# Block-sparse attention and an MLP in one kernel: the first loads, the sparse mask and the register load are given to other engines

## The chip, the cores and the metric

The kernel runs on one core of a Trainium2 chip. The metric is the time of one execution on the device, in microseconds (us); smaller is better. The core has TensorE (PE in the profile), VectorE (DVE), ScalarE (ACT), GpSimd (POOL) and SyncE (SP), which here does nothing but issue transfers (DMAs). Each engine runs its own instructions in the order of its program and waits on semaphores for the others. DMAs are issued by SyncE, GpSimd and, in the changed kernel, ScalarE.

## The reference

Four batches with eight heads each, 768 positions, 64 numbers per head. The positions are cut into 24 blocks of 32. A block of queries sees its own block and its two neighbours, the first and the last block, and three blocks drawn at random (`sampled_blocks`, 24 x 3). The first and the last block of queries see everything. The attention's output, 3072 tokens of 512 numbers, goes through an MLP.

```
scores = scale * q @ k.T                       # per batch and head, 768 x 768
mask   = window of 1 block | first, last block (rows and columns) | sampled blocks
attn   = softmax(where(mask, scores, -1e9))
x      = attn @ v                              # 3072 tokens x 512
r      = maximum(x @ w_in, 0)                  # 2048 wide
out    = (s * r * r + b) @ w_out               # 3072 x 512, f32
```

The inputs are in double precision; the kernel reads their words and, for the MLP's weights, takes the numbers apart on the chip (`decode_f64`).

## The kernel before, in words

**Order of the work.** The kernel first lists its steps as operations, `op(engine, cost, priority, function, ...)`, with what each needs, and a class `Plan` (line 109) then plays through them with a planned cost for each and writes every engine's program in the order in which the operations would start. The table `START` holds when an engine is assumed to begin, the table `T` due times. So a changed cost, priority or engine moves instructions far from the edit, while the work done stays the same.

**Two halves.** Index `e` is 0 or 1: each half takes two batches (a = 0, 1), with a key tile `kt0` or `kt1`. In each half the rows of queries are handled in slots: a dense slot (first and last block of queries, against all keys) and sparse sets 4s, 0s, 3s, 5s, 1s, 2s (the tile names `qr_4s` and so on; `qr_0d` holds the dense queries of a half). A query tile is loaded by four DMAs of 128 KB (`load_q`, line 711): two batches a by two halves par of the partitions. There are four buffers for query tiles. Sparse scores don't multiply with `kt` but with `kk`, a small tile of gathered key blocks, which GpSimd copies from `kt` (lines 894, 896, 905: window and global blocks; line 907: sampled blocks, at an address in a register).

**A slot.** TensorE multiplies queries and keys into a bank of scores (s, line 941 dense, line 962 sparse). VectorE takes scores, mask and the row's maximum (line 980, result nm). ScalarE takes the exponential (line 993). TensorE transposes the result (t, lines 1021 and 1023), VectorE or ScalarE copy it out (lines 1031, 1033, 1039, 1041), and TensorE multiplies with the values (xs, line 1089; od, line 1079) from tiles `vA` and `vB`, which SyncE and GpSimd load block by block (lines 769, 782 window blocks; 875, 879 sampled blocks).

**First loads.** SyncE loads the sampled numbers (`sbi`, line 808), four pieces of the keys (`kt`, line 703, 384 KB each), two of the four dense query loads (line 717), the other four pieces, the other two dense queries, and then values. GpSimd loads sparse queries: all four loads of a set before the key copies of its slot.

**Sampled numbers.** VectorE turns them into f32 (`sbf`, line 814) and packs the three of a query block into one word (`sparse_indices`, `packed`). GpSimd makes the mask of sampled blocks that the window or another sampled block already covers (`sparse_sampled`, 17 operations, shown as line 106, into `iv` and `mt`). SyncE and GpSimd then load the 22 words into registers (`load_registers`, line 850, one TENSOR_LOAD), and `block_register` shifts and masks one block number out of a word.

**In the middle.** While the attention runs, the MLP's weights `w_in` and `w_out` come in as `raw_i` and `raw_o` and are decoded in steps (lines 85 to 95: `wkhp`, `wklp`, `win`) that the plan puts between the others.

Of the kernel before, what the change touches and what calls it, by code (L numbers as in the profile page):

```python
# [19 lines left out]
P = 128  # L20
NEG = -float(2.0 ** 33)
# [87 lines left out]
class Plan:  # L109
# [7 lines left out]
    START = {"p": 1390.0, "a": 4000.0, "v": 2800.0, "g": 2130.0, "s": 600.0}  # L117
# [95 lines left out]
def kernel(  # L213
# [21 lines left out]
    NB = 24  # L235
# [430 lines left out]
    with ExitStack() as es:  # L666
# [44 lines left out]
        def load_q(key, a, par):  # L711
            kind, e, t = key
            if key not in qts:
                qts[key] = qp.tile([P, 2, NPAIR, P], F32, tag="qr", name=f"qr{e}_{t}{kind}")
            rows, b = slice(par * D, (par + 1) * D), 2 * e + a
            src = q_dup[b, t, rows, par::2, :] if kind == "s" and t < NSP else q_edge[b, int(kind == "d"), rows, par::2, :]
            (nc.gpsimd if kind == "s" else nc.sync).dma_start(out=qts[key][rows, a], in_=src)
# [86 lines left out]
        box = {}  # L804

        def load_sampled():
            box["sbi"] = ptp.tile([P, 4 * P], I32, tag="pt", name="sbi")[:, :2 * NB * NSL]
# [8 lines left out]
        packed = pers.tile([P, NB], I32, name="packed")  # L816

        def sparse_indices(V):

            cl = pers.tile([P, NB * NSL], F32, name="cl")  # L820
            V.tensor_scalar(out=cl, in0=sbf.rearrange("p a b -> p (a b)"), scalar1=0.0, scalar2=float(NB - 1), op0=ALU.max, op1=ALU.min)
            cv = cl.rearrange("p (n a) -> p n a", a=NSL)
            for a in range(1, NSL):
                V.scalar_tensor_tensor(out=cv[:, :, 0], in0=cv[:, :, a], scalar=float(NB32 ** a), in1=cv[:, :, 0], op0=ALU.mult, op1=ALU.add)
            V.tensor_copy(packed, cv[:, :, 0])

        iv = pers.tile([P, NB - 2, NSL], F32, name="iv")

        def sparse_sampled(G):

            t2 = pers.tile([P, NB - 2, NSL], F32, name="t2")
# [8 lines left out]
            for a in range(NSL):  # L840
                for c in range(a):
                    G.tensor_tensor(out=t2[:, :, 0], in0=sp[:, :, a], in1=sp[:, :, c], op=ALU.subtract)
                    G.tensor_scalar(out=t2[:, :, 0], in0=t2[:, :, 0], scalar1=0.0, scalar2=None, op0=ALU.is_equal)
                    G.tensor_tensor(out=iv[:, :, a], in0=iv[:, :, a], in1=t2[:, :, 0], op=ALU.add)
            G.tensor_scalar(out=mt[:, 1:NB - 1, 1:2 * NSL:2], in0=iv, scalar1=1.0, scalar2=NEG, op0=ALU.min, op1=ALU.mult)
# [3 lines left out]
        def load_registers(eng):  # L849
            _, regs[eng] = nc.values_load_multi_w_load_instructions(  # L850
                packed[0:1, 1:NB - 1], engines=[eng], min_val=0, max_val=NB32 ** NSL - 1, bass_reorder=False,
                skip_runtime_bounds_check_because="three numbers of 0..NB-1, clamped on the chip")

        def block_register(eng, k, a):

            n = regs[eng][k - 1] >> (5 * a) if a else regs[eng][k - 1]
            return (n & (NB32 - 1) if a < NSL - 1 else n).with_bounds(min_val=0, max_val=NB - 1)
# [298 lines left out]
        o_rg = op("g", 4800, T["RS"] - 2.0, lambda: load_registers(mybir.EngineType.Pool), [o_si])
# [23 lines left out]
        first_pk = first_q = pq = pvl = pvs = pk = o_m = o_e = o_rc = o_ev = None  # L1180
# [5 lines left out]
        for i, (kind, e, k, r) in enumerate(slots):  # L1186
# [4 lines left out]
            def queries(which=(0, 1), after=None):  # L1191
                nonlocal pq, first_q
                if which[0] in lqs.setdefault(qk, {}):
                    return
                if not dense:
                    first_q = first_q or qk
                for a in which:
                    for par in range(2):
                        fresh = not (a or par)
                        pq = op("s" if dense else "g", 450 if dense else 700, max(u - T["QL"], -18.0 if dense else -4.5) + 0.01 * par + (9.5 * (u == 0) if dense else 0.02) * a,  # L1200
                                lambda qk=qk, a=a, par=par: load_q(qk, a, par), alloc=[("qr", qk)] if fresh else [], use=[] if fresh else [("qr", qk)],
                                order=[pq] if dense else [pq, after, o_rg if first_q in (None, qk) else first_pk], nbytes=131e3)
                        lqs[qk].setdefault(a, []).append(pq)
# [412 lines left out]
```

## Time and profile before

| what | us |
|---|---|
| median of three runs | 764.71 |
| lowest and highest run | 760.99, 767.12 |
| span of the profiled execution, first to last instruction | 766.4 |
| TensorE busy in it | 739.7 |
| VectorE, ScalarE, GpSimd busy | 566.4, 475.0, 284.8 |

The profiled execution's own time is its span; the page gives nothing around it. Attention fills roughly the first 240 us, the MLP the rest. In the profile a group of equal instructions is one row: start, length, engine and line, operation, output and inputs, count; in square brackets stands the idle time of the engine just ahead of it and what ended it. "SPq" and "POOLq" are the engines' instruction queues, where the issue of a DMA shows.

### The profile page before, as it was taken

Reading aid. Unit: us, or ns where it says so; the run is one execution under the profiler, and the core shown is the slowest. Engines: PE = TensorE matmul, PEld = TensorE weight load, DVE = VectorE, ACT = ScalarE, POOL = GpSimd, SP = SyncE. Lnnn points to the kernel's source line nnn. Section 1 sums busy time; section 2 is a strip of 40 time slices with the busy share of each in tenths; the row PEclk is TensorE's granted clock in tenths of the full one; section 3 lists DMA queues with packets and bytes.
Section 4 is the critical chain, followed back from the end, with each engine's and each line's share of the span. In section 5 each row is a group of like instructions: output and inputs, shape, how many; then the busy total and the mean of one; then the engine's idle time right before and its main releaser. Section 6 shows DMA issues by size and latency. Waiting matters only on the chain.

```text
span 766.4 us, 21414 instructions
## 1 busy us (share of the span) xinstructions
PE 739.7 (97%) x8032; PEld 627.8 (82%) x8032; DVE 566.4 (74%) x1436; ACT 475.0 (62%) x1141; POOL 284.8 (37%) x477
## 2 busy tenths in 40 slices
PE   8899998999898999999999999999999999999997
PEld 6576676677677999998878899888888998888896
DVE  4766676988686898887896788796778678666652
ACT  3766677888686887879654444575444467345443
POOL 4866677566751221121032232233222232222221
PEclk9899999999999999999999999999999999999999
DMA  8787877756675335535532221224000022000002
GB/s 263 215 234 251 248 209 223 205 181 204 205 207 143 110 128 175 165 112 145 137 103 77 83 90 62 63 69 124 1 1 1 1 62 83 1 1 0 1 1 82
DMA packets 98743, 89.41 MB, mean 117 GB/s; under 512 B 50352, under 2 KB 79664, under 8 KB 98640
## 3 DMA queue, kind: packets, MB, share of 16 engines
q1 hardware_dynamic: 92544, 71.40, 31.1%
q0 software_dynamic: 6096, 16.65, 7.7%
q8 instruction: 63, 1.03, 0.6%
q14 instruction: 40, 0.33, 0.1%
HBM read 69.15 MB, written 14.68 MB: 109 GB/s over the span
## 4 chain that ended last, share of the span: by engine, by line
PE 80%; DVE 6%; ACT 5%; DMA 4%; issue 3%; SPq 1%; POOL 1%; POOLq 0%; ACTq 0%; DVEq 0%
PE m L622 20%; PE o L486 10%; PE o L487 10%; PE o L485 10%; PE xs L1089 5%; PE t L1023 5%; PE s L962 5%; PE h L443 3%; PE h L445 3%; PE h L444 3%; PE od L1079 2%; PE t L1104 2%; ACT ptile L993 1%; PE t L1021 1%; DVE ptile L980 1%
## 5 line engine op out<-in xcount | busy, mean ns | idle before, releaser
L464 POOL TENSOR_TENSOR hid<-hid,hid 128x384 fp32r<-128x384 f32 x96 | 105.6, 1101 | 292.6 <-ACT hid L640 248.9
L639 ACT ACTIVATE hid<-hid,sb_b,sb_s 128x384 f32<-128x384 f32 x96 | 68.0, 709 | 151.5 <-DVE hid L633 151.4
L993 ACT ACTIVATE ptile<-ptile,nm 128x256 f32<-128x256 f32 (+1 forms) x208 | 107.3, 520 | 35.3 <-DVE nm L980 35.2
L980 DVE CUSTOM_DVE_ANT_1 ptile<-s,mt 128x256 f32<-128x256 f32 x176 | 64.7, 420 | 28.0 <-PE s L962 27.8
L487 PE MATMUL o<-woutr,hid 128*128 128x512 f32 x168 | 66.5, 396 | 0.0
L486 PE MATMUL o<-woutr,hid 128*128 128x512 f32 x168 | 66.3, 395 | 0.0
L485 PE MATMUL o<-woutr,hid 128*128 128x512 f32 x168 | 65.3, 389 | 0.0
L622 PE MATMUL m<-wout,win 128*128 128x384 f32 x264 | 62.2, 339 | 1.1 <-ACT xrest L1509 0.6
L622 PE MATMUL m<-xp,wop 128*128 128x384 f32 x288 | 58.3, 337 | 0.0
L1023 PE MATMUL t<-ident,ptile 128*128 128x128 f32 x352 | 56.4, 301 | 1.6 <-issue 1.5
L486 PE MATMUL o<-win,hid 128*128 128x512 f32 x144 | 57.3, 398 | 0.0
L622 PE MATMUL m<-xp,win 128*128 128x384 f32 x288 | 55.7, 340 | 1.4 <-DVE xp L606 0.7
L633 DVE SCALAR_TENSOR_TENSOR hid<-hid 128x384 f32<-128x384 f32 x96 | 54.3, 566 | 3.3
L622 PEld LDWEIGHTS m<-xp,win 128*128 128x128 f32 x288 | 51.3, 189 | 4.6 <-DVE xp L606 1.2
L640 ACT CAST hid<-hid 128x384 fp32r<-128x384 f32 x96 | 49.3, 514 | 7.8 <-PE o L487 0.4
L1023 PEld LDWEIGHTS t<-ident,ptile 128*128 128x128 f32 x352 | 46.6, 209 | 8.8 <-issue 3.3
L622 PEld LDWEIGHTS m<-xp,wop 128*128 128x128 f32 x288 | 51.5, 188 | 2.1
L622 PEld LDWEIGHTS m<-wout,win 128*128 128x128 f32 x264 | 47.5, 188 | 3.5 <-ACT xrest L1509 1.0
L487 PE MATMUL o<-win,hid 128*128 128x512 f32 x126 | 50.1, 397 | 0.0
L485 PE MATMUL o<-win,hid 128*128 128x512 f32 x126 | 49.7, 394 | 0.2
L907 POOL COPY kk<-kt 128x256 f32 x132 | 49.8, 406 | 0.0
L1089 PE MATMUL xs<-vA,pt 128*32 128x64 f32 x1696 | 47.0, 227 | 2.1 <-DVE pt L1039 1.4
(195 smaller groups left out, 1868.1 us busy)
## 6 DMA issues: line engine op xcount, KB each, us to landing
vB<-in_v_dram SPq DMA_DIRECT2D x76, 128.0 KB, 3.7
raw_o<-in_w_out_dram SPq DMA_DIRECT2D x14, 512.0 KB, 3.3
raw_i<-in_w_in_dram SPq DMA_DIRECT2D x12, 512.0 KB, 3.8
vA<-in_v_dram POOLq DMA_DIRECT2D x46, 128.0 KB, 3.6
xd<-xst SPq DMA_DIRECT2D x44, 128.0 KB, 4.1
vA<-in_v_dram SPq DMA_DIRECT2D x42, 128.0 KB, 3.9
out_dram<-ob SPq DMA_DIRECT2D x20, 256.0 KB, 2.0
sum<-xd SPq DMA_DIRECT2D x12, 384.0 KB, 4.6
```

The lines of the kernel that those rows point to most:

```text
L464: (eng or nc.vector).tensor_tensor(out=htile(5 + i % 3), in0=t, in1=gh.bitcast(F32), op=ALU.subtract)
L485: nc.tensor.matmul(acc, gh[:, tsl], wout(f, 0), start=first, stop=False)
L486: nc.tensor.matmul(acc, gh[:, tsl], wout(f, 1), start=False, stop=False)
L487: nc.tensor.matmul(acc, gl[:, tsl], wout(f, 0), start=False, stop=last)
L622: nc.tensor.matmul(to, w_, x_, start=(c == 0 and k == 0), stop=(c == 1 and k == 2))
L633: vec.scalar_tensor_tensor(out=t, in0=t, scalar=0.0, in1=t, op0=ALU.max, op1=ALU.mult)
L639: nc.scalar.activation(t, t, AF.Identity, bias=sb_b, scale=sb_s)
L907: nc.gpsimd.tensor_copy(flat(kg[:, a:a + 1]), flat(kts[e][:, bass.ds(j, 1)]))
L980: nc.vector.tensor_tensor_reduce(out=pt, in0=sp, in1=msk, scale=-scale, scalar=FMAX if g == 0 else nm[:, 0:1], op0=ALU.add, op1=ALU.min, a ...
L993: nc.scalar.activation(pt, pt, AF.Exp, bias=nms[n][:, last:last + 1], scale=-1.0, accum_out=dns[i][:, g, j:j + 1])
L1023: nc.tensor.transpose(tp[:, (2 * j + c) * P:(2 * j + c + 1) * P], src[:, c:SW:2], ident)
L1089: nc.tensor.matmul(xs[quads[pair]], pt[:, c, quads[pair]], vt[:, a, col:col + D], start=(j == 0 and c == 0), stop=(c == 1), tile_position= ...
```

## The change

Five edits. `load_q` is told which engine issues: ScalarE the dense queries of the first half and the first sparse set, SyncE the dense queries of the second half, GpSimd the rest. Six block numbers instead of three stand in one word (`packs`), so that the register load reads 11 words. The mask is split: `sparse_near` (7 operations) stays on GpSimd, `sparse_same` (4) and `sparse_mask` (2) go to VectorE. GpSimd's queries of the next two sets get a priority and an order ahead of the key copies. `START["a"]`, the time from which the plan counts ScalarE as free, and planned costs are changed.

```
-    START = {"p": 1390.0, "a": 4000.0, "v": 2800.0, "g": 2130.0, "s": 600.0}
+    START = {"p": 1390.0, "a": 2400.0, "v": 2800.0, "g": 2130.0, "s": 600.0}
...
-        def load_q(key, a, par):
+        def load_q(key, a, par, on):
...
-            (nc.gpsimd if kind == "s" else nc.sync).dma_start(out=qts[key][rows, a], in_=src)
+            {"a": nc.scalar, "g": nc.gpsimd, "s": nc.sync}[on].dma_start(out=qts[key][rows, a], in_=src)
...
+        first = ptp.tile([P, 4 * P], I32, tag="pt", name="sbi")
+        box["sbi"], at_ = first[:, :2 * NB * NSL], [2 * NB * NSL]
...
-        packed = pers.tile([P, NB], I32, name="packed")
+        packed = room(NB)
+        packs = pers.tile([P, NB // 2 - 1], I32, name="packs")
...
+            V.scalar_tensor_tensor(out=packs, in0=packed[:, 2:NB - 1:2], scalar=5 * NSL, in1=packed[:, 1:NB - 2:2], op0=ALU.logical_shift_left, op1=ALU.bitwise_or)
...
-        def sparse_sampled(G):
+        def sparse_near(G):
...
-            for a in range(NSL):
-                for c in range(a):
-                    G.tensor_tensor(out=t2[:, :, 0], in0=sp[:, :, a], in1=sp[:, :, c], op=ALU.subtract)
-                    G.tensor_scalar(out=t2[:, :, 0], in0=t2[:, :, 0], scalar1=0.0, scalar2=None, op0=ALU.is_equal)
-                    G.tensor_tensor(out=iv[:, :, a], in0=iv[:, :, a], in1=t2[:, :, 0], op=ALU.add)
-            G.tensor_scalar(out=mt[:, 1:NB - 1, 1:2 * NSL:2], in0=iv, scalar1=1.0, scalar2=NEG, op0=ALU.min, op1=ALU.mult)
+        def sparse_same(V):
+            sp = sbf[:, 1:NB - 1]
+            V.tensor_tensor(out=same[:, :, 1:], in0=sp[:, :, 1:], in1=sp[:, :, :1].broadcast_to([P, NB - 2, 2]), op=ALU.subtract)
+            V.tensor_tensor(out=same[:, :, 0], in0=sp[:, :, 2], in1=sp[:, :, 1], op=ALU.subtract)
+            V.tensor_scalar(out=same, in0=same, scalar1=0.0, scalar2=None, op0=ALU.is_equal)
+            V.tensor_tensor(out=same[:, :, 2], in0=same[:, :, 2], in1=same[:, :, 0], op=ALU.add)
+        def sparse_mask(V):
+            V.tensor_tensor(out=iv[:, :, 1:], in0=iv[:, :, 1:], in1=same[:, :, 1:], op=ALU.add)
+            V.tensor_scalar(out=mt[:, 1:NB - 1, 1:2 * NSL:2], in0=iv, scalar1=1.0, scalar2=NEG, op0=ALU.min, op1=ALU.mult)
...
-                packed[0:1, 1:NB - 1], engines=[eng], min_val=0, max_val=NB32 ** NSL - 1, bass_reorder=False,
+                packs[0:1], engines=[eng], min_val=0, max_val=NB32 ** (2 * NSL) - 1, bass_reorder=False,
...
-            n = regs[eng][k - 1] >> (5 * a) if a else regs[eng][k - 1]
-            return (n & (NB32 - 1) if a < NSL - 1 else n).with_bounds(min_val=0, max_val=NB - 1)
+            n, at = regs[eng][(k - 1) // 2], a + (k - 1) % 2 * NSL
+            n = n >> (5 * at) if at else n
+            return (n & (NB32 - 1) if at < 2 * NSL - 1 else n).with_bounds(min_val=0, max_val=NB - 1)
...
-        o_rs = op("s", 4400, T["RS"], lambda: load_registers(mybir.EngineType.SP), [o_si])
-        o_rg = op("g", 4800, T["RS"] - 2.0, lambda: load_registers(mybir.EngineType.Pool), [o_si])
+        o_rs = op("s", 2400, T["RS"], lambda: load_registers(mybir.EngineType.SP), [o_si])
+        o_rg = op("g", 2600, T["RS"] - 2.0, lambda: load_registers(mybir.EngineType.Pool), [o_si])
...
+                on = "a" if qk in (("d", 0, 0), first_q) else "s" if dense else "g"
+                soon = sum(x[0] == "s" for x in lqs) <= 3
...
-                        pq = op("s" if dense else "g", 450 if dense else 700, max(u - T["QL"], -18.0 if dense else -4.5) + 0.01 * par + (9.5 * (u == 0) if dense else 0.02) * a,
-                                lambda qk=qk, a=a, par=par: load_q(qk, a, par), alloc=[("qr", qk)] if fresh else [], use=[] if fresh else [("qr", qk)],
-                                order=[pq] if dense else [pq, after, o_rg if first_q in (None, qk) else first_pk], nbytes=131e3)
+                        pq = pqs[on] = op(on, {"s": 450, "a": 620, "g": 650}[on], max(u - T["QL"], -18.0 if dense else -9.0 if soon else -4.5) + 0.01 * par + 0.02 * a,
+                                lambda qk=qk, a=a, par=par, on=on: load_q(qk, a, par, on), alloc=[("qr", qk)] if fresh else [], use=[] if fresh else [("qr", qk)],
+                                order=[pqs.get(on)] if on != "g" else [pqs.get(on), after, o_rg if soon else first_pk], nbytes=131e3)
```

TensorE's program is the same before and after, row by row. The other engines' programs change at these places.

ScalarE at its start, before. `ptile` is the tile of exponentials, `nm` the negated maximum, and L993 the exponential:

```order
L790 ACT_TABLE_LOAD
L790 ACTIVATE warm_108<-ident_101 128x1 [waits Pool_49]
L993 ACTIVATE ptile2_79,dn0_262<-ptile2_79,nm0_249 128x128x3 [waits DVE_49]
L993 ACTIVATE ptile6_80,dn0_262<-ptile6_80,nm0_249 128x128x3
L993 ACTIVATE ptile6_80,dn0_262<-ptile6_80,nm1_259 128x128x3 [waits DVE_49]
```

And after, where L1010 is the exponential; DMAHW0 to DMAHW7 are the eight semaphores that the DMAs of SyncE and ScalarE use in turn (`sbi` has 0, the key pieces have 1 to 7 and then 0):

```order
L790 ACT_TABLE_LOAD
L790 ACTIVATE warm_108<-ident_101 128x1 [waits Pool_49]
L717 DMA qr0_0d_134<-in_q_edge_dram 64x4x128 [waits DMAHW1_49]
L717 DMA qr0_0d_134<-in_q_edge_dram 64x4x128 [waits DMAHW2_49]
L717 DMA qr0_0d_134<-in_q_edge_dram 64x4x128 [waits DMAHW4_49]
L717 DMA qr0_0d_134<-in_q_edge_dram 64x4x128 [waits DMAHW5_49]
L717 DMA qr0_4s_170<-in_q_dup_dram 64x4x128 [waits DMAHW6_49]
L717 DMA qr0_4s_170<-in_q_dup_dram 64x4x128 [waits DMAHW0_49]
L717 DMA qr0_4s_170<-in_q_dup_dram 64x4x128 [waits DMAHW1_49]
L717 DMA qr0_4s_170<-in_q_dup_dram 64x4x128 [waits DMAHW2_49]
L1010 ACTIVATE ptile2_79,dn0_252<-ptile2_79,nm0_238 128x128x3 [waits DVE_49]
```

Eight DMA instructions, each with a wait, stand ahead of ScalarE's first exponential.

GpSimd in the middle, before, around the load of `qr1_0s` (the second half's 0s queries) and the weight copies `wklp`:

```order
L879 DMA vB_232<-in_v_dram 32x2x512
L717 DMA qr1_0s_2607<-in_q_dup_dram 64x4x128 x4
L782 DMA vA_231<-in_v_dram 32x2x512
L894 COPY kk_301<-kt1_590 128x256
L896 COPY kk_301<-kt1_590 128x768
```

And after, from the window copy that follows the three slots' first copies:

```order
L896 DMA vA_161<-in_v_dram 32x2x512
L913 COPY kk_278<-kt1_522 128x256
L922 COPY kk_278<-kt1_522 128x256
...
L924 COPY kk_278<-kt1_522 128x256
L88 COPY wklp0_524<-raw_o0_2450 128x512
L717 DMA qr1_0s_3036<-in_q_dup_dram 64x4x128 x4
L717 DMA qr1_3s_3059<-in_q_dup_dram 64x4x128 x4
```

The second half's 0s and 3s queries have moved behind the first slots' key copies and behind the copy `wklp<-raw_o`.

VectorE in the middle, before, where `xss` closes a slot and L980 is the maximum of the next dense slot:

```order
L1031 TENSOR_SCALAR dp_2715<-t_0_2699,kept 128x4x128
L1095 TENSOR_TENSOR xss_2732<-od_796,rc_452 128x128
L85 TENSOR_SCALAR wkhp_431<-raw_o_2496 128x512
L980 ISA ptile_80,nm_2748<-s_0_2723,mz 128x128x3
L980 ISA nm_2748 128x1
```

And after, at the same place (L997 is the maximum):

```order
L1048 TENSOR_SCALAR dp_2669<-t_0_2654,kept 128x4x128
L1112 TENSOR_TENSOR xss_2686<-od_756,rc_418 128x128
L93 TENSOR_TENSOR win_2690<-wkhp_396,raw_i_2248 128x512
L997 ISA ptile_80,nm_2700<-s_0_2677,mz 128x128x3
L997 ISA nm_2700 128x1
```

The step on `raw_o` no longer stands there; it comes 44 rows later.

## Rows read from the trace of the kernel before

**Rows 1.** The page's first part: busy time, share of the span and instructions of each engine.

```profile
PE 739.7 (97%) x8032; PEld 627.8 (82%) x8032; DVE 566.4 (74%) x1436; ACT 475.0 (62%) x1141; POOL 284.8 (37%) x477
```

**Rows 2.** Windows of 40 us: the window and its length, busy time of PE, PEld, DVE, ACT and POOL with the number of instructions, the granted TensorE clock, the DMA share and GB/s.

```profile
0.00:40.00 40.00, 33.72 (x360) 24.58 (x368) 24.29 (x88) 21.75 (x64) 27.49 (x77) 0.92 0.81 236
...
120.00:160.00 40.00, 36.26 (x735) 25.94 (x723) 33.55 (x120) 33.05 (x102) 26.09 (x53) 0.96 0.71 203
```

**Rows 3.** Timeline of SyncE's queue: its first load of sampled values.

```profile
23.62 0.64 SPq L879 DMA_DIRECT2D vA<-in_v_dram  x1
```

**Rows 4.** Timeline of VectorE and ScalarE at the start of the dense stage: the first maximum and two exponentials.

```profile
11.86 0.56 DVE L980 CUSTOM_DVE_ANT_1 ptile<-s,mz 128x384 f32<-128x384 f32 x1 [5.77 <-PE s L941]
...
13.23 0.61 ACT L993 ACTIVATE ptile<-ptile,nm 128x384 f32<-128x384 f32 x1 [10.87 <-DVE nm L980]
...
16.07 0.62 ACT L993 ACTIVATE ptile<-ptile,nm 128x384 f32<-128x384 f32 x1 [0.28 <-DVE nm L980]
```

**Rows 5.** Timeline of TensorE in the dense stage and around 34 us.

```profile
10.84 2.80 PE L941 MATMUL s<-kt,qr_0d 64*64 64x384 f32 x28 [1.24 <-DMA qr_0d<-in_q_edge_dram]
...
17.22 1.74 PE L941 MATMUL s<-kt,qr_0d 64*64 64x384 f32 x16
...
21.61 1.78 PE L941 MATMUL s<-kt,qr_0d 64*64 64x384 f32 x16
...
32.21 0.76 PE L962 MATMUL s<-kk,qr_3s 64*32 64x256 f32 x16
34.54 1.56 PE L962 MATMUL s<-kk,qr_3s 64*32 64x256 f32 x16 [1.57 <-DMA qr_3s<-in_q_dup_dram]
36.03 1.93 PE L1089 MATMUL xs<-vA,pt 128*32 128x64 f32 x64
37.89 1.98 PE L1023 MATMUL t<-ident,ptile 128*128 128x128 f32 x8
```

**Rows 6.** The chain that ended last, in order of time, from 26 to 48 us: start, length, what.

```profile
28.41 6.09 DMA qr_3s<-in_q_dup_dram
...
41.72 1.03 PE xs L1089 x64
...
43.83 1.15 PE t L1023 x8
```

**Rows 7.** Windows, columns as in rows 2.

```profile
4.00:18.00 14.00, 12.06 (x95) 9.60 (x93) 6.22 (x23) 4.49 (x14) 6.19 (x19) 1.00 1.10 323
34.00:40.00 6.00, 5.46 (x96) 3.87 (x104) 2.89 (x12) 1.20 (x6) 4.07 (x11) 0.50 0.74 215
130.00:132.00 2.00, 2.00 (x33) 0.76 (x21) 1.60 (x6) 0.82 (x4) 0.15 (x1) 0.50 0.39 93
```

**Rows 8.** Timeline of VectorE, GpSimd and TensorE around 128 us.

```profile
127.29 0.43 DVE L85 TENSOR_SCALAR wkhp<-raw_o 128x512 int32<-128x512 int32 x1 [2.71 <-DMA raw_o<-in_w_out_dram]
127.64 0.55 DVE L980 CUSTOM_DVE_ANT_1 ptile<-s,mz 128x384 f32<-128x384 f32 x1
...
127.32 1.01 POOL L88 COPY wklp<-raw_o 128x512 uint16<-128x512 uint16 x1 [0.20 <-DMA raw_o<-in_w_out_dram]
...
128.34 0.64 PE L962 MATMUL s<-kk,qr_2s 64*32 64x256 f32 x8 [1.64 <-POOL wklp L88]
129.59 1.93 PE L962 MATMUL s<-kk,qr_2s 64*32 64x256 f32 x24 [0.62 <-DVE nm L980]
...
131.86 1.60 PE L1089 MATMUL xs<-vA,pt 128*32 128x64 f32 x64
```

**Rows 9.** Timeline of GpSimd: four query loads of the front, a value load, and the loads of the second half's 0s queries.

```profile
22.29 2.44 POOL L717 DMA_DIRECT2D qr_0s<-in_q_dup_dram  x4
...
38.08 0.55 POOL L782 DMA_DIRECT2D vA<-in_v_dram  x1 [1.40 <-PE xs L1089]
...
119.79 2.47 POOL L717 DMA_DIRECT2D qr_0s<-in_q_dup_dram  x4 [0.83 <-PE t L1104]
```

**Rows 10.** The tiles kt and qr_0d in the first 20 and 30 us, and line 850, the register load: instructions with their least, median and greatest duration in ns and first and last start; and the time from a DMA's issue to its landing (the first such row is that of kt, the second that of qr_0d).

```profile
L703 SPq DMA_DIRECT2D kt<-in_k_blk_dram x8: 422/578/2332, 1.3 to 9.9; - x8
...
DMA to landing us min/median/max: 4.7/5.7/6.9
...
L717 SPq DMA_DIRECT2D qr_0d<-in_q_edge_dram x4: 603/846/1092, 5.3 to 12.5; - x4
...
DMA to landing us min/median/max: 4.6/5.4/5.4
...
L850 POOLq TENSOR_LOAD <-packed x1: 5151/5151/5151, 11.2 to 11.2; - x1
```

**Rows 11.** Timeline of GpSimd and TensorE from 139 to 153 us.

```profile
139.69 0.39 POOL L896 COPY kk<-kt 128x256 f32<-128x256 f32 x1 [2.33 <-PE s L962]
...
140.37 1.09 POOL L907 COPY kk<-kt 128x256 f32 x3
...
146.66 1.46 PE L962 MATMUL s<-kk,qr_0s 64*32 64x256 f32 x32
...
151.68 1.09 PE L962 MATMUL s<-kk,qr_3s 64*32 64x256 f32 x32
```

**Rows 12.** The tiles qr_0s and qr_3s from 110 to 140 us: the time from issue to landing of the second half's loads (the first row is that of qr_0s).

```profile
DMA to landing us min/median/max: 5.1/5.2/5.3
...
DMA to landing us min/median/max: 3.8/3.8/3.8
```

More of the change, by code (lines that the diff above doesn't have):

```diff
@@ L804, with room @@
         box = {}
+        first = ptp.tile([P, 4 * P], I32, tag="pt", name="sbi")
+        box["sbi"], at_ = first[:, :2 * NB * NSL], [2 * NB * NSL]
+        def room(n):
+            at_[0] += n
+            return first[:, at_[0] - n:at_[0]]
         def load_sampled():
-            box["sbi"] = ptp.tile([P, 4 * P], I32, tag="pt", name="sbi")[:, :2 * NB * NSL]
             nc.sync.dma_start(
@@ L814, in sampled_blocks @@
             V.tensor_copy(sbf.rearrange("p a b -> p (a b)"), box["sbi"].rearrange("p (n two) -> p n two", two=2)[:, :, 0])
-        packed = pers.tile([P, NB], I32, name="packed")
+        packed = room(NB)
+        packs = pers.tile([P, NB // 2 - 1], I32, name="packs")
         def sparse_indices(V):
-            cl = pers.tile([P, NB * NSL], F32, name="cl")
+            cl = room(NB * NSL).bitcast(F32)
             V.tensor_scalar(out=cl, in0=sbf.rearrange("p a b -> p (a b)"), scalar1=0.0, scalar2=float(NB - 1), op0=ALU.max, op1=ALU.min)
@@ L825, in sparse_indices @@
             V.tensor_copy(packed, cv[:, :, 0])
+            V.scalar_tensor_tensor(out=packs, in0=packed[:, 2:NB - 1:2], scalar=5 * NSL, in1=packed[:, 1:NB - 2:2], op0=ALU.logical_shift_left, op1=ALU.bitwise_or)
         iv = pers.tile([P, NB - 2, NSL], F32, name="iv")
-        def sparse_sampled(G):
-            t2 = pers.tile([P, NB - 2, NSL], F32, name="t2")
+        same = room((NB - 2) * NSL).bitcast(F32).rearrange("p (n a) -> p n a", a=NSL)
+        def sparse_near(G):
+            t2 = room((NB - 2) * NSL).bitcast(F32).rearrange("p (n a) -> p n a", a=NSL)
             sp, own = sbf[:, 1:NB - 1], jf[:, 1:NB - 1].unsqueeze(2).broadcast_to([P, NB - 2, NSL])
@@ L850, in load_registers @@
             _, regs[eng] = nc.values_load_multi_w_load_instructions(
-                packed[0:1, 1:NB - 1], engines=[eng], min_val=0, max_val=NB32 ** NSL - 1, bass_reorder=False,
-                skip_runtime_bounds_check_because="three numbers of 0..NB-1, clamped on the chip")
+                packs[0:1], engines=[eng], min_val=0, max_val=NB32 ** (2 * NSL) - 1, bass_reorder=False,
+                skip_runtime_bounds_check_because="six numbers of 0..NB-1, clamped on the chip")
         def block_register(eng, k, a):
-            n = regs[eng][k - 1] >> (5 * a) if a else regs[eng][k - 1]
-            return (n & (NB32 - 1) if a < NSL - 1 else n).with_bounds(min_val=0, max_val=NB - 1)
+            n, at = regs[eng][(k - 1) // 2], a + (k - 1) % 2 * NSL
+            n = n >> (5 * at) if at else n
+            return (n & (NB32 - 1) if at < 2 * NSL - 1 else n).with_bounds(min_val=0, max_val=NB - 1)
         ring = {"k": {}, "v": {}}
@@ L1147, in chain @@
             for step in later.steps:
-                dep = op(eng, cost, prio, step, [dep])
+                dep = op(eng, cost, prio, step, [dep], use=[("pt", "sbi")])
             return dep
         o_si = chain("v", nc.vector, 250, T["SI"], sparse_indices, o_sb)
-        o_ss = chain("g", nc.gpsimd, 270, T["MS2"], sparse_sampled, o_sb)
-        o_rs = op("s", 4400, T["RS"], lambda: load_registers(mybir.EngineType.SP), [o_si])
-        o_rg = op("g", 4800, T["RS"] - 2.0, lambda: load_registers(mybir.EngineType.Pool), [o_si])
+        o_sn = chain("g", nc.gpsimd, 330, T["MS2"], sparse_near, o_sb)
+        o_sd = chain("v", nc.vector, 200, T["SI"] + 0.1, sparse_same, o_sb)
+        o_ss = op("v", 450, T["SI"] + 0.2, lambda: sparse_mask(nc.vector), [o_sn, o_sd], use=[("pt", "sbi")])
+        o_rs = op("s", 2400, T["RS"], lambda: load_registers(mybir.EngineType.SP), [o_si])
+        o_rg = op("g", 2600, T["RS"] - 2.0, lambda: load_registers(mybir.EngineType.Pool), [o_si])
         kld = {}
@@ L1179 @@
         devs, drc, done, late, held, pav = {}, {}, {}, {}, set(), None
-        first_pk = first_q = pq = pvl = pvs = pk = o_m = o_e = o_rc = o_ev = None
+        pqs = {}
+        first_pk = first_q = pvl = pvs = pk = o_m = o_e = o_rc = o_ev = None
         lastk = {}
@@ L1191, in queries @@
             def queries(which=(0, 1), after=None):
-                nonlocal pq, first_q
+                nonlocal first_q
                 if which[0] in lqs.setdefault(qk, {}):
```

## The prediction, made before the changed kernel was run

> **What bounds the kernel now.** I read the page's busy times first: TensorE works 739.7 us of a span of 766.4 us [rows 1]. In stretches of 40 us it works 33.72 us of the first and 36.26 of the fourth [rows 2]. So a microsecond that TensorE loses anywhere is a microsecond of the end, and a faster loading front counts only as far as it takes idle time or the lower clock away from TensorE. The timelines of those two stretches then show three losses.
>
> First, the start. The first dense scores run at 10.84, 1.24 us after the warm-up ended [rows 5], and ScalarE, idle for 10.87 us, begins its first exponential at 13.23 [rows 4]. From there the dense stage goes at the pace of ScalarE and VectorE.
>
> Second, the stop at 33 us. The second half of the first qr_3s scores waits 1.57 us for its query load, issued by GpSimd as late as 28.41 behind the key copies [rows 5, 6]. The granted clock is then 0.50 from 34 to 40 us, the 1.2 GHz level [rows 7]. That costs more than the wait: 1.56 us for 16 scores that take 0.76 before it, 1.93 for 64 xs and 1.98 for 8 t that take 1.03 and 1.15 a few us later [rows 5, 6], together 0.80 + 0.90 + 0.83 = 2.5. The place loses 1.6 + 2.5 = 4.1 us.
>
> Third, 127 us. VectorE stands 2.71 us at wkhp<-raw_o, a step of the MLP weight decoding, until a load lands; the maxima of the next dense slot are queued behind it. TensorE waits 1.64 and 0.62 us [rows 8] and runs at a clock of 0.50 again [rows 7].
>
> **The change, part by part.**
>
> *ScalarE issues eight query loads.* All stand in its in-order program ahead of the first exponential. The order printed for the changed program says what each waits for: eight DMA semaphores are used in turn by the loads of SyncE and ScalarE, and a load takes its semaphore only when the load before it on that one has landed. Counted off, sbi has 0, key pieces 1 to 7 have 1 to 7, and key piece 8, which itself waits for sbi, has 0 again. ScalarE's fourth dense load therefore waits for the fifth key piece, the first qr_4s load for the sixth, and the second qr_4s load, on semaphore 0, for the eighth and last. That a DMA instruction holds its engine while it waits is seen on GpSimd: a vA load at 38.08 has 1.40 us of idle time ahead of it, put down to TensorE's xs [rows 9]. So the first exponential starts after the last key piece has landed, plus three issues.
>
> The Trainium skill says the same: by "DMA: Bandwidth & Descriptors", section "Anatomy of one DMA — SWDGE (gpsimd) path", DMA engines do not wait on semaphores; the issuing sequencer waits before it dispatches. The trace agrees, by the 1.40 us of GpSimd just named.
>
> When does that piece land? From 4 to 18 us the engines moved 323 GB/s at a DMA share of 1.10 [rows 7]: issuing earlier finds no free transfer time. Before, the last key issue starts at 9.9 and a piece lands after 4.7 to 6.9 us [rows 10], so at 14.6 to 16.8. After, ahead of its landing go 8 keys of 0.393 MB, sbi 0.074, four dense queries of 0.131, one qr_4s of 0.131, one vA of 0.131: 4.0 MB, and of GpSimd's eight early loads 0 to 0.7 MB. At 0.323 MB/us from 4 us on, 4.0 to 4.7 MB end at 16.4 to 18.6. I take 17, and as the early end 15.6, with keys, sbi and dense queries alone. ScalarE has issued no DMA in the trace; GpSimd's issues take 0.61 each (2.44 for four) [rows 9], SyncE's dense queries up to 1.09 [rows 10]. I take GpSimd's, since by then no key is left to issue: 17 + 0.1 + 3 x 0.62 = 19.0, against 13.23. That is +5.8 us (+4.3 from 15.6 and 0.61, +8.7 from 18.6 and 1.09). Whether the first scores come a little earlier is then worth nothing: what follows them waits for the exponentials.
>
> The rule against this part stands in the Trainium skill, page "DMA: Bandwidth & Descriptors", section "Issuing engines are not separate DMA queues": several issuing engines save only the sequencer's issue time. The DMA share of 1.10 agrees. By it alone the sum of this part would be about 0, not +5.8; the waits make the difference.
>
> Two small terms follow. VectorE is by then ahead, so the 0.28 us that ScalarE waited at 16.07 [rows 4] goes: -0.3. And TensorE, its score banks full after some 3 us, stands still for about 6; no row shows so long a stop, and after the 1.57 us at 34 the clock fell. From one dense slot's 16 scores to the next are 4.4 us (17.22 to 21.61 [rows 5]), in which TensorE has little idle time; at half clock a slot is up to 4 us longer. The half clock at 34 held for some 6 us: I take half a slot's price, +2 (0 if the clock doesn't fall, +4 for a whole slot).
>
> *GpSimd loads qr_0s and qr_3s ahead of the copies; mask on two engines; short register load.* Before, GpSimd's load of 22 words begins at 11.2, behind 17 mask operations, and takes 5.15 us [rows 10]. With ten operations fewer it begins no later; 11 words take an estimated 2.6, eight issues 4.9, so the last is out by 18.7 and, with the 6.1 us of [rows 6], landed by 24.8, long before the qr_3s scores, which stood at 32 and come some 8 us later. The wait and its clock go: -4.1 (0 if another wait takes the place). The key copies begin with the last key piece at 17 or behind these issues; one slot's copies fit between the end of its four issues (22.29 + 2.44 [rows 9]) and 28.41, where the next set is already being issued [rows 6], so three take under 11 us and end by 30, wanted one slot after the other from about 33 on: hidden. VectorE's six mask operations lie in its 5.77 us before the first maximum [rows 4]: hidden. SyncE's vA and sampled loads now wait for qr_4s to land, near 22; its first sampled load went out at 23.62 [rows 3], so little is late.
>
> Front: +5.8 - 0.3 + 2 - 4.1 = +3.4.
>
> *The middle, moved by the plan.* The other engines' programs are reordered, TensorE's is the same row by row. At VectorE's place of wkhp<-raw_o stands win<-wkhp,raw_i, which waits for no load but those of the first keys; the raw_o step comes 44 rows later. VectorE was free at 124.58 (127.29 less 2.71), so with one step ahead the dense maxima start at about 125.6 instead of 127.64, the x24 scores near 127.4 instead of 129.59 (-2.2), and without half clock they take 0.8 (24 of the 32 in 1.09 us of [rows 11]) instead of 1.93 and the next 64 xs 1.03 instead of 1.60 [rows 6, 8]: -1.1 - 0.6. Sum -3.9 (0 if win waits as long; -4.4 if no idle time is left).
>
> But GpSimd's loads of qr_0s and qr_3s for the second half (e = 1) move too, from ahead of the copies, at 119.79 [rows 9], to behind them. They now follow five copies that wait for TensorE's first e = 1 qr_4s scores (139.69, [rows 11]) and the copy wklp<-raw_o of 1.01 us [rows 8]. Kept in the clock of before: copies from 139.69 to 141.45, wklp to 142.46, issues start at 142.46, 143.08, 143.70, 144.32. Query loads in this stretch landed after 3.8 to 5.3 us [rows 12]: the second at 146.9 to 148.4, the fourth at 148.1 to 149.6. TensorE wants the first pair at 146.66 and the second about half a microsecond later [rows 11]. The end of these scores slips by 0.9 to 2.4 us; I take 1.6, and half of the 2.5 that the clock cost at 34 us, since of the two stops nearest in size, 1.24 and 1.57 us, one was followed by the lower clock and one not: +2.9 (0.9 to 4.9). qr_3s lands by 152, wanted at 151.68 plus this delay: hidden.
>
> Middle: -3.9 + 2.9 = -1.0.
>
> **Sum.** +3.4 - 1.0 = +2.4 us on the profiled span, 768.8. The page gives no time around the span; the span lies 1.7 above the median of the runs (764.71; 760.99 to 767.12). On the median the sum is 767.1, said as 767. A measurement of this kernel tells about 1%, 7.6 us, from no change: this is none.
>
> **Rivals.**
>
> *A, faster:* ScalarE's waits do not hold the exponentials, because the last key lands near 13, or a waiting load does not stop what is behind it. For it: DMA issues are not engine work in the profile. Against: GpSimd's 1.40 us [rows 9]. First exponential then at most about 1.4 later (the second dense load, issued at 7.1, lands after 4.6 to 5.4 us [rows 10], against 10.84 for the first scores), front 1.4 - 0.3 - 4.1 = -3.0; with no wait at 146 and no idle time left at 127 the middle is -4.4: -7.4, 757.3. Chance 0.11.
>
> *B, slower:* the hold is longer. It decides from a first exponential at 22 us on: last key at 18.6, three issues at 1.09, as SyncE's were while the engines were full, and TensorE at half clock for a whole dense slot. Front +8.7 - 0.3 + 4 - 4.1 = +8.3, with the middle +7.3; with the dear end of the wait at 146 (4.9) +9.3: 772.0 to 774.0. Chance 0.22.
>
> *C, the stall moves:* the stop at 33 us stays in another form (key copies or value loads late), 4.1 is not gained: +6.5, 771.2. For it: SyncE's value loads now wait for qr_4s. Against: the xs that use them are at 36 and later. Chance 0.07.
>
> The forecast, 0.60, goes from -4 to +6.5. With A to 757.3 and B to 774.0, and 2 us more for the spread of the runs, the range is 758 to 776; A's edge is left out. Faster by over 1% is most of A (0.08), slower by over 1% the upper half of B and C with some of the forecast's edge (0.20); the rest, 0.72, within 1%.
>
> **What the profile of after would show.** Right: ScalarE's first exponential at 17 to 22 us with some 15 us idle ahead, TensorE idle for 4 to 8 us and a granted clock of 0.50 in the dense stage; no wait for qr_3s behind it; no wait of VectorE for raw_o near 127; a wait of TensorE for qr_0s some 7 us after the first e = 1 qr_4s scores. Wrong: a first exponential before 15 (A), a full clock through the dense stage, a new wait for kk or vA before 45 (C), or a total beyond 758 to 776.

## The result, and the profile after

| | before | after |
|---|---|---|
| median of 14 runs each, us | 765.03 | 771.82 |
| lowest and highest run | 760.79, 767.35 | 765.30, 773.87 |
| span of the first profiled execution | 766.4 | 768.9 |
| TensorE busy in it | 739.7 | 740.7 |

The ratio is 1.0089, 95% interval 1.0067 to 1.0112: slower by 0.9%, inside the 1% that the forecast called no change, and at its upper edge; 771.8 against the 767 forecast, in the range of 758 to 776. The two profiles differ by 2.5 us, the forecast by 2.4; the medians differ by 6.8. The text below has to explain both. In every run on record the time is 1.6 to 1.7 us longer than the span, so a span is not yet the execution's time. The medians and ratios below leave out one execution of e1_again (3951 us) and one of e5_hold_before (1417 us). The ratios come from runs of the kernel before in the same series (medians 763.87 to 766.21) and differ from the quotient of the medians by up to 0.3%, so differences of that size mean little.

ScalarE at the start of the changed kernel (answers to [rows 4]):

```profile
5.99 5.56 ACTq L717 DMA_DIRECT2D qr_0d<-in_q_edge_dram  x4
13.42 8.16 ACTq L717 DMA_DIRECT2D qr_4s<-in_q_dup_dram  x4
21.63 0.61 ACT L1010 ACTIVATE ptile<-ptile,nm 128x384 f32<-128x384 f32 x1 [19.27 <-DMA qr_4s<-in_q_dup_dram]
```

Its four qr_4s loads take 8.16 us to issue, though one issue takes some 0.6, and the first exponential comes at 21.63 instead of 13.23. The first of them goes out at 13.42, 0.02 us after the sixth key piece has landed; the second at 19.71, 0.02 us after the eighth. The chain that ended last runs through just this place: a key load, the qr_4s issue, the exponential.

```profile
6.41 6.99 DMA kt<-in_k_blk_dram
13.40 0.02 issue
13.42 8.21 DMA qr_4s<-in_q_dup_dram
21.63 0.00 issue
21.63 0.72 ACT ptile L1010 x2
```

The key tile and its landings in the first 22 us (answers to [rows 10]):

```profile
L703 SPq DMA_DIRECT2D kt<-in_k_blk_dram x8: 418/1046/2300, 1.3 to 8.6; - x8
...
DMA to landing us min/median/max: 4.7/6.5/11.1
```

The last piece is issued at 8.6 instead of 9.9 and lands 11.1 us later, at 19.7, instead of at most 16.8. It is issued earlier and lands later. What the DMA engines moved until then (columns as in [rows 7]) is 292 GB/s, against the 323 of before from 4 to 18 us:

```profile
4.00:19.70 15.70, 11.64 (x71) 7.29 (x69) 5.29 (x22) 0.00 (x0) 8.48 (x17) 0.78 1.15 292
```

TensorE, before (two rows that [rows 5] does not show) and after:

```profile
25.94 1.22 PE L962 MATMUL s<-kk,qr_4s 64*32 64x256 f32 x32
...
39.80 1.54 PE L962 MATMUL s<-kk,qr_4s 64*32 64x256 f32 x32
```

```profile
13.75 5.38 PE L958 MATMUL s<-kt,qr_0d 64*64 64x384 f32 x28 [0.58 <-DMA qr_0d<-in_q_edge_dram]
22.39 3.75 PE L1038 MATMUL t<-ident,ptile 128*128 128x128 f32 x16 [3.26 <-ACT ptile L1010]
...
34.91 1.22 PE L979 MATMUL s<-kk,qr_4s 64*32 64x256 f32 x32
...
41.02 1.09 PE L979 MATMUL s<-kk,qr_3s 64*32 64x256 f32 x32
42.05 1.10 PE L1106 MATMUL xs<-vA,pt 128*32 128x64 f32 x64
...
44.23 1.09 PE L979 MATMUL s<-kk,qr_4s 64*32 64x256 f32 x32
```

It waits 3.26 us for ScalarE, works at half clock (28 dense scores in 5.38 us against 2.80), and reaches the sparse scores at 34.91 instead of 25.94. The qr_3s scores no longer wait; xs, at 36.03 before, is 6.0 late, and the next slot's scores (44.23 against 39.80) 4.4. Windows of the changed kernel, columns as in [rows 7], show the clock low in the dense stage and full where it was 0.50:

```profile
22.00:26.00 4.00, 3.61 (x16) 3.03 (x16) 1.95 (x7) 3.94 (x13) 4.00 (x10) 0.57 1.11 290
...
34.00:40.00 6.00, 5.63 (x88) 3.93 (x88) 5.78 (x23) 6.00 (x19) 3.12 (x9) 1.00 1.00 264
```

The middle (answers to [rows 8] and [rows 11]), TensorE, VectorE and GpSimd:

```profile
122.61 0.44 PE L1121 MATMUL t<-ident,xss 128*128 128x128 f32 x2 [1.48 <-DVE pt L1056]
...
129.92 1.51 PE L979 MATMUL s<-kk,qr_2s 64*32 64x256 f32 x32
...
148.67 0.97 PE L979 MATMUL s<-kk,qr_0s 64*32 64x256 f32 x8 [0.56 <-DMA qr_0s<-in_q_dup_dram]
...
127.79 0.69 DVE L93 TENSOR_TENSOR win<-wkhp,raw_i 128x512 fp32r<-128x512 f32 x1
...
141.88 2.46 POOL L717 DMA_DIRECT2D qr_0s<-in_q_dup_dram  x4
```

VectorE does not wait for raw_o; the 32 qr_2s scores run in one piece of 1.51 us. The qr_0s loads go out at 141.88 and their scores wait, for 0.56 us and then at a lower clock. Not foreseen: a wait of 1.48 us at 122.61 for VectorE's copy of pt.

### The profile page after: what moved, and what is told of

Read it like the earlier page. It is cut to its first block, busy times and chain, and to the rows that moved or that the text cites. A ratio compares the mean times of both kernels' runs of the same rounds, so it can differ in the third digit from the quotient of the medians.

```text
span 768.9 us, 21535 instructions
## 1 busy us (share of the span) xinstructions
PE 740.7 (96%) x8032; PEld 627.5 (82%) x8032; DVE 566.6 (74%) x1443; ACT 474.0 (62%) x1141; POOL 280.2 (36%) x463
## 4 chain that ended last, share of the span: by engine, by line
PE 83%; DVE 6%; ACT 4%; DMA 3%; issue 2%; SPq 1%; ACTq 0%; DVEq 0%
PE m L622 20%; PE o L486 10%; PE o L487 10%; PE o L485 10%; PE t L1040 6%; PE s L979 6%; PE xs L1106 6%; PE h L443 3%; PE h L445 3%; PE h L444 3%; PE od L1096 2%; PE t L1121 2%; PE t L1038 2%; DMA qr_4s<-in_q_dup_dram 1%; PE s L958 1%
## 5 line engine op out<-in xcount | busy, mean ns | idle before, releaser
L1010 ACT ACTIVATE ptile<-ptile,nm 128x256 f32<-128x256 f32 (+1 forms) x208 | 107.3, 520 | 42.8 <-DVE nm L997 23.4
L997 DVE CUSTOM_DVE_ANT_1 ptile<-s,mt 128x256 f32<-128x256 f32 x176 | 64.4, 421 | 27.3 <-PE s L979 27.1
```

Source lines behind the costliest of these rows:

```text
L997: nc.vector.tensor_tensor_reduce(out=pt, in0=sp, in1=msk, scale=-scale, scalar=FMAX if g == 0 else nm[:, 0:1], op0=ALU.add, op1=ALU.min, a ...
L1010: nc.scalar.activation(pt, pt, AF.Exp, bias=nms[n][:, last:last + 1], scale=-1.0, accum_out=dns[i][:, g, j:j + 1])
```

## The experiments

Three theories were on trial. H: ScalarE's hold at the front costs the time. Q: GpSimd's early query loads crowd the keys out of the DMA engines. M: the middle costs it. Each kernel edits the list of operations that the plan hands out, so that only the instructions named move, or changes one line.

**The changed kernel again (e1_again).** No edit.

> The changed kernel once more, unchanged, for a second profile beside its times. The median of the runs lies 6.8 us above the kernel before, while the two profiles taken so far differ by 2.5 us only. Theory H (the loss is ScalarE's hold at the front): the first exponential again starts at 21 to 22.5 us, and the shift of TensorE against the profile of before is about +9 us at the first sparse scores and +4 us at 48 us. Theory M (the loss comes from the middle): the front gives the same +4, but other places between 60 and 245 us lose 2 to 4 us more than in the first profile. Total 770 to 773 in both.

768.59 us (769.46 with the execution left out), ratio 1.0081 (1.0041 to 1.0121), span 766.7; the expected 770 to 773 is missed by 1.4. First exponential at 21.14, TensorE 9.1 us late at the sparse scores, 4.6 at the following slot, and the same waits of 1.48 and 0.56 us in the middle.

```profile
21.14 0.62 ACT L1010 ACTIVATE ptile<-ptile,nm 128x384 f32<-128x384 f32 x1 [18.78 <-DMA qr_4s<-in_q_dup_dram]
```

The front repeats; M has no place of its own. The end does not repeat: this span is only 0.3 us above that of before, because TensorE, 2.9 us late at 190 us, has caught up by 210; in that stretch the profile of before has stops of 1.17 and 1.54 us with no releaser named.

**Hold alone (e5_hold_before).** In the kernel before, ahead of its first exponential:

```
+        plan.hold = lambda key: nc.scalar.activation(warm, qts[key][:, 1, NPAIR - 1, :1], AF.Exp)
... run just ahead of the first exponential, with the key of the qr_4s set
```

> The kernel before with one instruction added: ahead of its first exponential ScalarE reads one number of the last load of the first sparse query set, which GpSimd issues near 19 us. Nothing else moves. Theory H: the first exponential starts near 22.5 us instead of 13.2, TensorE comes 9 us late to the sparse scores, the wait for qr_3s at 33 us (4 us) is covered by that, and the sum is +4 to +6 us: 769 to 771. Theory M or Q: a late ScalarE alone costs under 2 us, since the dense stage has slack: 765 to 767.

770.70 us, 1.0083 (1.0052 to 1.0113), as H said. The added instruction waits for the load and everything follows:

```profile
22.59 0.20 ACT L1510 ACTIVATE warm<-qr_4s 128x1 f32<-128x1 f32 x1 [20.23 <-DMA qr_4s<-in_q_dup_dram]
22.70 0.60 ACT L1032 ACTIVATE ptile<-ptile,nm 128x384 f32<-128x384 f32 x1
```

One late instruction on ScalarE, with all loads and the middle as before, costs as much as the whole change.

**No loads on ScalarE (e2_no_scalar).** In the changed kernel:

```
-            {"a": nc.scalar, "g": nc.gpsimd, "s": nc.sync}[on].dma_start(out=qts[key][rows, a], in_=src)
+            (nc.gpsimd if kind == "s" else nc.sync).dma_start(out=qts[key][rows, a], in_=src)
... the dense loads' operations are put behind the 4th and 8th key piece, qr_4s ahead of qr_0s
```

> The changed kernel with ScalarE's eight query loads given back: the dense queries to SyncE between the key pieces, as before, the first sparse set to GpSimd ahead of its other early loads. All else stays, GpSimd's early loads and the order of every other instruction too. Theory H: the first exponential starts at 13 to 14.5 us, the qr_3s wait stays away, so the front is 4 us better than before and 8 us better than the changed kernel: 759 to 763 us. Theory Q (not the hold, but GpSimd's early loads crowd the key loads): the last key piece still lands near 19.7, the dense slots wait for their keys, and the time stays at 767 to 771. Theory M: 769 to 772, since the middle is that of the changed kernel.

768.97 us, 1.0038 (1.0012 to 1.0063): H's 759 to 763 is missed by 6. The hold is gone, but not the delay (timelines of ScalarE and TensorE):

```profile
13.28 0.62 ACT L1034 ACTIVATE ptile<-ptile,nm 128x384 f32<-128x384 f32 x1 [10.92 <-DVE nm L1021]
...
25.76 0.62 ACT L1034 ACTIVATE ptile<-ptile,nm 128x384 f32<-128x384 f32 x1 [6.00 <-DVE nm L1021]
...
18.99 0.86 PE L982 MATMUL s<-kt,qr_0d 64*64 64x384 f32 x4 [1.65 <-DMA qr_0d<-in_q_edge_dram]
21.09 2.83 PE L982 MATMUL s<-kt,qr_0d 64*64 64x384 f32 x12 [1.24 <-DMA qr_0d<-in_q_edge_dram]
```

The first exponential is at 13.28, and then the second pair of dense queries lands late and ScalarE stands 6 us in the midst of the dense stage. Twelve loads of GpSimd, the first of them wanted for the sparse scores only, share the DMA engines with them. Theory Q is right beside H.

**ScalarE's loads ahead of its table load (e3_table_later).** The eight issues come first and take other semaphores, so that they wait for early loads only.

```
-        nc.scalar.activation(warm, ident[:, :1], AF.Exp)
+        plan.warm = lambda: nc.scalar.activation(warm, ident[:, :1], AF.Exp)
... run behind the last of the eight loads; the dense loads' operations are put behind the 2nd key piece, qr_4s behind the 8th
```

> The changed kernel with ScalarE's eight loads issued ahead of its table load and warm-up instead of behind them. The same loads by the same engine; but they then take their semaphores ahead of the keys, and wait for sbi, the first dense load and two early key pieces only. Theory H (the hold is the wait for the last key piece): ScalarE is free by 10 us, the first exponential at 13 to 15 us, 759 to 764 us. Theory I (eight issues on ScalarE cost as such): first exponential at 16 us or later, 766 us or more. Theory Q: as H for ScalarE, but dense scores wait for keys, 766 to 770.

770.17 us, 1.0077 (1.0047 to 1.0106). ScalarE is free at 11.5, but the first exponential waits until 17.32, since the keys now come late:

```profile
15.07 4.39 PE L983 MATMUL s<-kt,qr_0d 64*64 64x384 f32 x24 [4.69 <-DMA kt<-in_k_blk_dram]
23.37 0.88 PE L983 MATMUL s<-kt,qr_0d 64*64 64x384 f32 x8 [1.02 <-DMA kt<-in_k_blk_dram]
25.58 0.88 PE L983 MATMUL s<-kt,qr_0d 64*64 64x384 f32 x8 [1.33 <-DMA kt<-in_k_blk_dram]
```

The theory that eight issues cost as such falls, since ScalarE is free at 11.5. H's time is missed too, but the hold has not gone; it has moved to SyncE, whose key loads now come behind ScalarE's in the turn of the semaphores. SyncE's key issues, the last of which starts at 8.6 in the changed kernel, stretch to 13.5, and SyncE waits ahead of them (its waits up to 30 us: what waited for what, us in total, times, longest):

```profile
L729 SPq DMA_DIRECT2D kt<-in_k_blk_dram x8: 368/502/2668, 1.3 to 13.5; - x8
...
SPq L729 <- DMA kt<-in_k_blk_dram: 5.1, 2, 4.6
SPq L729 <- DMA qr_0d<-in_q_edge_dram: 2.9, 2, 2.2
```

How much of the keys' delay is this, and how much is crowding (landings took up to 12.0 us), the run does not separate.

**GpSimd's loads late, ScalarE's kept (e6_late_gpsimd).**

```
... the qr_0s loads' operations are put ahead of the 0s slot's key copies, the qr_3s loads' ahead of the 3s slot's
```

> The changed kernel, in which GpSimd issues the loads of qr_0s and qr_3s where the kernel before has them, each set ahead of its own slot's key copies; ScalarE keeps its eight loads. Theory H+Q (ScalarE's hold, made longer by GpSimd's early loads, which share the DMA engines with the keys): the last key piece lands at 16.5 to 17.5 instead of 19.7, the first exponential starts near 19 instead of 21.6, TensorE reaches the sparse scores 2 to 3 us earlier, 766.5 to 769. Theory H alone (the early loads do not matter): 21 to 22 us again, 769 to 772.

769.04 us, 1.0068 (1.0035 to 1.0102), where the ranges of both theories meet. The profile tells them apart. The second qr_4s load, which waits for the last key piece, goes out at 16.95 instead of 19.71; that piece, issued at 8.8, so landed within 8.2 us, not 11.1. The first exponential is at 18.87, as H+Q said:

```profile
18.87 0.61 ACT L1035 ACTIVATE ptile<-ptile,nm 128x384 f32<-128x384 f32 x1 [16.51 <-DMA qr_4s<-in_q_dup_dram]
```

With GpSimd's early loads it was at 21.63 and 21.14, so 2.3 to 2.8 us of the hold are theirs.

**Both undone (e7_order_of_need).** The dense loads as in e2_no_scalar; qr_4s, qr_0s and qr_3s behind the first slot's key copies.

> The changed kernel with ScalarE's loads given back to SyncE, in the places of the kernel before, and GpSimd's three sets (4s, 0s, 3s) issued behind the first slot's key copies, which themselves wait for the keys. So no query that is needed late is issued while keys and dense queries are on their way. Theory H+Q: dense stage as before (first exponential at 13.3, sparse scores at 26), and no wait for qr_3s behind it: the front is 4 us better than before, the middle about 0 to +1, 761 to 763, ratio 0.995 to 0.998. Theory M (the middle costs several us): 765 or more.

763.78 us, 1.0018 (0.9987 to 1.0049): the loss is gone, but H+Q's ratio of 0.995 to 0.998 is not reached. The front is what the change might have had (TensorE):

```profile
25.65 1.22 PE L1007 MATMUL s<-kk,qr_4s 64*32 64x256 f32 x32
...
31.76 1.09 PE L1007 MATMUL s<-kk,qr_3s 64*32 64x256 f32 x32
32.78 1.10 PE L1134 MATMUL xs<-vA,pt 128*32 128x64 f32 x64
...
34.97 1.09 PE L1007 MATMUL s<-kk,qr_4s 64*32 64x256 f32 x32
```

No wait for qr_3s; the next slot's scores at 34.97 instead of 39.80 are 4.8 us early, and the span, 761.4, is 5.0 below that of before. Yet the median is that of before. Either the 4.8 us are not in most runs of before, or something takes them back; the next kernels ask which.

**The middle as well (e8_middle_too).** The second half's dense queries are loaded behind the 2s queries, and its 0s queries as soon as the buffer is free.

> As the kernel that loads in the order of need, and in the middle the dense queries of the second half are loaded behind the 2s queries instead of ahead of the 1s queries. The buffer that the second half's 0s queries wait for is then the one of the first half's 1s queries, and they are issued some 20 us earlier. Theory W (the wait for qr_0s near 148 costs 1.2 to 2.5 us as in the two profiles of the changed kernel): that wait is gone, 758.5 to 761.5, ratio near 0.993, below both other kernels. Rival: the wait is hidden behind others, no change against the kernel that loads in the order of need.

765.32 us, 1.0040 (1.0011 to 1.0069): no gain, so W's 758.5 to 761.5 is missed. The loads go out at 116.1 instead of 134.7, the wait of 1.14 us that the kernel just above has for them is gone, and a wait a few us on has grown from 1.58 to 1.81:

```profile
147.64 0.44 PE L1152 MATMUL xs<-ident,xss 128*128 128x128 f32 x2 [1.81 <-DVE xss L1143]
```

VectorE, with three steps of weight decoding ahead of xss, is the next to be late.

**The stop at 33 us alone, taken away and made longer (e9_qr3s_alone, e10_qr3s_late).** In the kernel before, the qr_3s loads are put ahead of the 0s slot's key copies, or behind those of their own slot.

> The kernel before with four loads moved: GpSimd issues qr_3s right behind qr_0s, ahead of the 0s slot's key copies, some 2.5 us earlier. Nothing else. Theory S (the stop at 33 us costs 4 us, most of it by the clock): landing at 30 to 32.5 instead of 34.5, the wait of 1.57 us shrinks to 0 to 0.5, the clock stays at 1.00, but the copies of the 0s slot come 2.4 us later, at the moment of their need: -2.5 to -4 us, 761 to 762.5. Rival: the late copies make a wait of the same size, 764 to 766.

> The kernel before with GpSimd's four qr_3s loads moved the other way, behind the key copies of their own slot: issued from 29.7 instead of 27.2. Theory S (the stop is in every execution, and a later load makes it longer): wait of 3 to 4 us instead of 1.57, half clock as before or longer, +2.5 to +4 us on the median. Theory V (in most executions the load lands in time or nearly): +1 to +2.5 us.

Taken away: 764.58 us, 1.0006 (0.9975 to 1.0038), inside the rival's 764 to 766. Its profile has no wait for qr_3s, a full clock, and the following scores at 36.53 instead of 39.80, but also, as the rival said, a wait for the late copies:

```profile
29.87 1.19 PE L986 MATMUL s<-kk,qr_0s 64*32 64x256 f32 x32 [0.79 <-POOL kk L931]
...
36.53 1.09 PE L986 MATMUL s<-kk,qr_4s 64*32 64x256 f32 x32
```

This profiled execution, 768.65 us, was the longest of the run's ten. Made later: 767.37, 1.0026 (0.9996 to 1.0056), with waits of 1.24 and 0.25 us: S's +2.5 to +4 us are not there. Neither moves the median beyond its interval.

**The kernel before twice more (b1_before_again, b2_before_again).** No edit; one execution each.

> The kernel before once more, for a second profile. Its profiled execution took about 3 us more than the median of its runs, which range from 758 to 769. Theory V (the stop at 33 us differs from execution to execution, and the profile caught a dear one): a profiled execution near 762 to 765 shows a shorter wait for qr_3s or a full clock behind it, and a dear one shows what the first profile shows. Rival: the stop is the same 4 us in every execution and the spread comes from other places between 40 and 245 us.

> As the run of the kernel before just ahead of it, a third profile: theory V wants the stop at 33 us to follow the time; the rival wants the stop to stay and TensorE's other stops to follow it.

Spans 762.6 and 759.5, against 766.4 of the profile that the prediction was read from. TensorE and the window from 34 to 40 us in the first of the two:

```profile
34.11 0.64 PE L962 MATMUL s<-kk,qr_3s 64*32 64x256 f32 x8 [0.18 <-DMA qr_3s<-in_q_dup_dram]
...
36.87 1.09 PE L962 MATMUL s<-kk,qr_4s 64*32 64x256 f32 x32
...
34.00:40.00 6.00, 5.89 (x202) 4.47 (x204) 4.87 (x24) 4.92 (x19) 5.36 (x14) 1.00 0.79 243
```

and in the second, with VectorE's raw_o step:

```profile
32.21 0.64 PE L962 MATMUL s<-kk,qr_3s 64*32 64x256 f32 x8 [0.22 <-POOL kk L907]
33.40 2.26 PE L962 MATMUL s<-kk,qr_3s 64*32 64x256 f32 x24 [0.56 <-DMA qr_3s<-in_q_dup_dram]
...
38.61 1.09 PE L962 MATMUL s<-kk,qr_4s 64*32 64x256 f32 x32
...
34.00:40.00 6.00, 6.00 (x125) 3.69 (x122) 3.33 (x13) 2.48 (x8) 4.47 (x12) 0.72 0.76 231
...
123.63 0.43 DVE L85 TENSOR_SCALAR wkhp<-raw_o 128x512 int32<-128x512 int32 x1 [1.46 <-DMA raw_o<-in_w_out_dram]
```

From the first 4s scores to the second, 13.86 us in the profile read (25.94 to 39.80), it takes 10.12 (26.75 to 36.87) and 12.80 (25.81 to 38.61) here, and 9.32 in e7_order_of_need, which has no stop. Against that the stop costs 4.5, 0.8 and 3.5 us. VectorE's wait for raw_o is 2.71, none and 1.46 us. Theory V holds for both stops. It is not the whole spread: the second execution, 1.7 us behind the first at the second 4s scores, ends 3.1 us ahead of it.

## Why the prediction was right, and where it was not

*The hold.* Right in mechanism: ScalarE's second qr_4s load goes out when the last key piece has landed, and the first exponential follows. Too small in size: 19.0 was forecast, 21.63 and 21.14 came. The step that failed is the landing, 17 with 18.6 as its end: 19.7. Two terms of it were mis-sized. The bytes: 292 GB/s over 15.7 us are 4.6 MB, near the upper end of the 4.0 to 4.7, so by this count most of GpSimd's early loads went ahead; at 323 GB/s they would have been through at 18.2, some 1.2 us after the forecast. The rate, taken from before: 292 instead of 323 is worth the other 1.5. e6_late_gpsimd, without the early loads, has 18.87, near the forecast, though its rate from 4 to 18 us is low too (293). What lowers the rate is not shown.

*The clock in the dense stage*, +2: it fell, to 0.57 over 22 to 26 us, and ahead of the stop already: it was 0.50 from 14 to 18 us, after TensorE had waited 2.90 us for the first dense queries. Hold and clock made the sparse scores 9.0 us late, where +5.8 - 0.3 + 2 = +7.5 stood.

*The stop at 33 us*, -4.1: in the profile it was worth 4.5, so that the front came out at +4.4 by the next slot, where +3.4 was forecast.

*Between front and middle* nothing was forecast, and TensorE's delay fell by 2.7, from 4.4 us to 1.7 at the dense scores of 113 us (114.95 against 113.22). Of this 1.9 goes near 72 us, where TensorE stops in the profile of before, with no releaser named, and not in that of after (chain of before):

```profile
70.67 1.53 issue
72.20 0.40 PE s L962
```

*The middle*, -1.0: from 1.7 us late at 113 to 1.9 late at 156 (156.57 against 154.70), so +0.1. In it the raw_o stop gave 4.0 (-3.9 forecast), the wait for qr_0s took 2.9 by the qr_3s scores (153.93 against 151.68; +2.9 forecast), of which 0.4 came back, and the unforeseen wait for pt took 1.5. Behind it another 0.6 was lost.

Sum of the profiles: +4.4 - 2.7 + 0.1 + 0.6, near +2.5, forecast +2.4. That the two agree is luck: front, middle and what came behind were 2.7 us above their terms, and 2.7 us in a stretch without a term made up for it.

*The median*, +6.8: here the base failed. The prediction took the span of 766.4 for the time and so placed it 1.7 us above the median. With the 1.6 to 1.7 us that every run has around its span, that execution took some 768.0, 3.0 above the median of 765.0; the profiled execution of the changed kernel took 770.57, 1.3 below its median. 2.5 + 3.0 + 1.3 is the 6.8. The -4.1 and -3.9 were priced from that dear execution of before, in which both stops were long, and then set against the median. Two further profiles have them at 0.8 and 3.5, and at none and 1.46 us of wait; against their spans that of the changed kernel is 6.3 and 9.4 us longer, not 2.5. What a change takes away counts with its usual size: taken away alone, the stop at 33 us changed the median by 0.06% (-0.25 to +0.38). The hold is in both profiles of the changed kernel, and alone it costs +0.83%. So the loss is near the hold's whole price, not near +2.4. Undone, both parts of the front bring the median back to that of before.

*Rivals.* B, the longer hold, came nearest: its price was 772.0 to 774.0, with the first exponential from 22 us on; but what made the hold longer was the late landing, not slow issues, which took ScalarE 0.54 to 0.64 us each. A fell: a waiting DMA does hold what stands behind it. C fell: nothing waits before 45 us in the place of qr_3s.

Open: how much of the change's loss is crowding and how much hold in the median (each undone alone leaves 0.38% and 0.68%, with intervals of 0.3% to either side), whether the rest of the change takes back some of what the stops are worth on the mean (e7_order_of_need has none of the 33 us stop and is not faster; its span of 761.4 lies between those of the two later profiles of before), and what ends TensorE's stops near 70 and 195 us, for which the profile names no releaser.

## What to carry to other kernels

A DMA in a compute engine's program is a wait in that program: look up which earlier DMA its semaphore belongs to, and put nothing urgent behind it; moved to the front, the same loads made SyncE's keys wait instead (e3_table_later). While the DMA engines were full, as here, issuing a load earlier moved another one back, so issue in the order of need. And before a stop is counted as a gain, compare the profiled execution's time, not its span, with the median, and see whether a second profile has the stop: a gain priced from one execution is worth only what it has on the mean, while a wait that is built in is paid every time.

## What the runs showed of the hardware

ScalarE's DMA issues, which no row had shown, took 0.54 to 0.64 us. Landing times stretched when more engines issued: a key piece took up to 6.9 us with SyncE alone, 11.1 with three engines issuing, at most 8.2 with GpSimd's loads taken back (e6_late_gpsimd). And the same stop of one program, 0.18, 0.56 and 1.57 us of waiting for one load in three executions, went with a mean granted clock of 1.00, 0.72 and 0.50 from 34 to 40 us, and cost 0.8, 3.5 and 4.5 us.
